# All steps of the kernel traced in one explicit order under a manual schedule

## The chip, the cores and the metric

The kernel runs on one NeuronCore of one Trainium2 chip, as one program with one launch. The metric is the device time of that core in microseconds (us); the time of a kernel is the median of several executions. The engines are TensorE (PE, with its weight loads listed apart as PEld), VectorE (DVE), ScalarE (ACT), GpSimd (POOL) and SyncE (SP), whose queue here issues all transfers. Each engine works through its own queue of instructions in order; between engines there are only semaphores.

## The reference

Three layers follow each other, for 8 independent batches of 576 positions and 512 channels (8 heads of 64):

```
# 1. attention over a memory of 32 slots per head
a    = softmax(phi, over the 576 positions)              # phi: 8 heads x 576 x 32
k_m, v_m = a^T k, a^T v                                  # 32 x 64 per head
x    = softmax(q k_m^T / 8) v_m                          # 576 x 64 per head, heads side by side
# 2. a mix over positions of rank 32, then an MLP, both with a residual
u    = x + (x^T U V)^T
y    = u + max(u w_ch1, 0) w_ch2                         # 512 -> 2048 -> 512
# 3. causal attention of 4 experts with 64 channels each, the two best by a gate
w    = softmax over the 2 largest of y w_gate, else 0
out  = sum_e w_e * (softmax(causal(q_e k_e^T / 8)) v_e wo_e),   q_e, k_e, v_e = y wq_e, y wk_e, y wv_e
```

Inputs and output are float32. The kernel writes every float32 operand of a matmul as the sum of two float16 numbers, hi and lo, and forms each product as hi*hi + hi*lo + lo*hi, so that one product of the reference is three matmuls.

## The kernel before, in words

**Steps.** The work of one batch is cut into steps, which are Python functions; most are generators, and what lies between two `yield` statements is a *segment*: a few instructions, mostly of one engine. Stage 1 (L542) has for each of four pairs of heads `pair_max`, `pair_scale`, `pair_hl` (the split into hi and lo, L661 to L673), `pair_qT` (a transposing DMA), `pair_kv` (L693), `pair_kb`, `pair_scores` (L729), `soft_a` and `soft_b`, and for each two pairs `half_t` (a transposing DMA), `half_p` and `half_a` (L904); `u_max` (L971) ends it with the largest magnitude over the whole tile. Such a maximum over all rows goes through PE each time: DVE fills a diagonal (L246) and a matmul with ones spreads it (L256, named `ur` after `u_max`, `ar` after `pair_max`, `yr` after `y_max`). `u_scale` and `a_split` scale and split the result, `u_mm` (L1054) forms u, and `zed` (L1078) folds the first weights of the MLP with the values of stage 1 so that the batches 1 to 7 need fewer products in `up`.

`mlp` (L1111) goes twice through 8 units of `up` (L1136, into one PSUM bank each, evicted as a hi part by ACT L1138 and a lo part by DVE L1140) and 4 of `down` (L1150, added to u by DVE L1157) for each half of the positions. `stage2` (L1178) takes the maximum (`y_max`), scales and splits y (`y_split`, L1230), and projects it (`proj` L1240, `vg` L1276). For each of five tiles of 128 positions and each pair of experts, `unit_s` forms scores on PE, then DVE masks them and takes their minimum (L1364), ACT takes the exponential (L1370) and a float16 copy (L1371), POOL forms the lo part (L1373), and SP issues a transposing DMA (L1375); `unit_v` (L1428) multiplies by the values, `unit_o` scales and transposes the result, `unit_w` (L1507) projects it and ACT evicts it (L1515).

**Buffers.** PSUM has three pools of banks: three banks with tag m (L175) for `up` and `down`, four with tag a (L178) for nearly everything else, and one with tag v (L181) for `unit_v`. A step that needs a bank waits until the one traced before it in that pool's ring has been read.

**Stages.** From the start the weights are loaded, converted and split (`w1_conv`, `w1_split`, `w2_conv`, `w2_split`, `sw_max`, `sw_split`) while batch 0 runs through stage 1 and its MLP. From then on a period holds `mlp` of batch b, `stage2` of batch b-1, and stage 1 of batch b+1, all mixed. In the end the MLP of batch 7 runs beside stage 2 of batch 6, and stage 2 of batch 7 runs alone.

**What sets the order.** Two things, one after the other. First a heap of events (`at` L1585, `run` L1589): each step gets a modelled time by hand (the constants UNIT, T0, LEAD, ZT, U_MM), and its segments are traced in the order of these times, each `yield` giving how much later the next segment follows. In the first part some weight steps are pinned behind the main work with `issue_after`. Then the framework's planner takes the traced instructions and reorders them in each engine's queue, by its own model of durations. The two last batches are traced from a text of step names, `ORDER2` (L1561, L1698 to L1702), and that part too goes through the planner. Where six matmuls in a row should stay in their order, as in `u_mm` and in the scores, the helper `in_order` (L305) chains them with `issue_after`, and the two banks of such a pair are taken in reversed order (`[::-1]`).

Of the kernel before, what the change touches and what calls it, by code (L numbers as in the profile page):

```python
# [53 lines left out]
ORDER2 = """  # L54
vg.P.0 y_max.P y_max.P y_scale.P y_scale.P y_split.P.0.0 y_split.P.0.0 y_split.P.0.3 y_split.P.0.3 y_split.P.1.2
y_split.P.1.2 y_scale.P y_split.P.0.2 y_split.P.1.3 up.0.0 up.0.1 up.0.0 up.0.0 up.0.1 y_split.P.1.0 y_split.P.0.1
y_split.P.0.1 up.0.1 up.0.2 up.0.3 y_split.P.0.2 up.0.2 up.0.2 y_split.P.1.0 u_mm.0.0 u_mm.0.0 u_mm.0.1 u_mm.0.1 up.0.4
up.0.4 proj.P.1.0.0 proj.P.1.0.0 up.0.3 proj.P.1.0.0 up.0.5 proj.P.0.0.0 up.0.4 up.0.3 up.0.5 proj.P.1.0.0 up.0.5 up.0.6
up.0.7 down.0.0.0.0 up.0.6 up.0.6 vg.P.1 up.0.7 up.0.7 down.0.0.0.1 down.0.0.1.0 y_split.P.1.1 y_split.P.1.1
y_split.P.1.3 proj.P.1.0.1 down.0.0.1.1 down.0.0.2.0 proj.P.1.0.1 vg.P.2 proj.P.0.0.0 vg.P.1 down.0.0.0.1 down.0.0.1.1  # L60
proj.P.0.0.0 down.0.0.2.1 vg.P.1 down.0.0.3.0 vg.P.2 vg.P.0 proj.P.1.0.0 proj.P.1.0.1 down.0.0.3.1 unit_s.P.0.0.0 vg.P.4
vg.P.2 vg.P.0 proj.P.1.0.1 proj.P.1.0.1 unit_s.P.0.0.1 vg.P.4 unit_s.P.0.0.0 unit_s.P.0.0.0 unit_s.P.0.0.0 vg.P.0 vg.P.3
vg.P.3 vg.P.3 down.0.0.3.1 down.0.0.2.1 unit_s.P.0.0.1 unit_s.P.0.0.1 unit_s.P.0.0.0 unit_s.P.0.0.0 proj.P.0.0.1 up.1.0
up.1.1 up.1.0 vg.P.4 unit_s.P.0.0.0 unit_s.P.1.0.0 proj.P.0.0.1 proj.P.0.0.1 up.1.2 up.1.1 unit_s.P.0.0.1 unit_s.P.0.0.1
unit_s.P.0.0.1 up.1.0 gate.P unit_o.P.0.0 unit_s.P.1.0.1 up.1.3 unit_s.P.1.0.0 up.1.1 unit_s.P.1.0.0 unit_s.P.1.0.0
up.1.2 up.1.2 unit_s.P.1.0.1 gate.P gate.P unit_o.P.0.0 gate.P unit_s.P.0.0.1 u_mm.1.0 u_mm.1.0 u_mm.1.1 u_mm.1.1 up.1.4
up.1.3 gate.P unit_v.P.0.0.0 up.1.3 up.1.4 up.1.5 unit_s.P.2.0.1 up.1.5 up.1.4 gate.P up.1.5 up.1.6 up.1.6 up.1.7 up.1.7
down.1.0.0.0 up.1.6 up.1.7 unit_s.P.3.0.0 unit_s.P.2.0.1 unit_s.P.2.0.1 gate.P unit_s.P.1.0.0 unit_s.P.1.0.0
unit_s.P.1.0.0 gate.P gate.P down.1.0.0.1 down.1.0.0.1 down.1.0.1.0 unit_v.P.0.0.1 unit_s.P.1.0.1 down.1.0.1.1
down.1.0.2.0 unit_s.P.1.0.1 unit_s.P.3.0.0 gate.P unit_o.P.0.0 unit_s.P.2.0.1 unit_o.P.0.0 unit_s.P.3.0.0 unit_s.P.1.0.1  # L70
unit_s.P.1.0.1 unit_v.P.1.0.0 down.1.0.1.1 unit_s.P.1.0.1 down.1.0.2.1 down.1.0.3.0 unit_s.P.2.0.0 unit_o.P.0.0
unit_s.P.2.0.0 unit_v.P.1.0.1 down.1.0.3.1 unit_s.P.3.0.1 unit_s.P.2.0.0 unit_s.P.2.0.0 unit_s.P.2.0.0 down.1.0.3.1
unit_s.P.2.0.0 unit_s.P.2.0.0 down.1.0.2.1 up.0.8 up.0.8 unit_s.P.2.0.1 unit_s.P.2.0.1 up.0.8 unit_s.P.3.0.1
unit_o.P.1.0 unit_o.P.1.0 up.0.9 up.0.9 up.0.9 unit_o.P.0.0 unit_o.P.1.0 unit_o.P.1.0 unit_o.P.1.0 up.0.10 up.0.10
unit_s.P.3.0.1 unit_o.P.2.0 unit_o.P.2.0 up.0.11 unit_v.P.2.0.0 up.0.11 up.0.11 unit_s.P.3.0.0 unit_s.P.3.0.0 up.0.10
# [74 lines left out]
def kernel(ctx: ExitStack, tc: tile.TileContext, q, k, v, phi, U, V, w1, w2, wg, wq, wk, wv, wo, out):  # L150
# [154 lines left out]
    def in_order(calls):  # L305
        last = None
        for f in calls:
            with tc.issue_after(last) if last is not None else nullcontext():
                f()
# [1430 lines left out]
```

## Time and profile before

| | |
|---|---|
| median of 3 runs | 1311.68 us (1308.8 to 1317.54) |
| the profiled execution's own time | 1309.13 us |
| its span, first to last instruction | 1307.1 us |
| mean granted clock of PE, 1 is full speed | 0.956 |
| busy share of the span: PE, DVE, ACT, POOL | 88%, 72%, 60%, 31% |
| DMA | 137.8 MB, 105 GB/s on average |

The durations quoted further on all come from the profiled execution, 2.6 us under the median. A busy engine is one that executes an instruction, so 88% says that PE had nothing to execute in 12% of the span; it does not say that the matmuls ran at the highest speed, since the granted clock sets their pace. PEld is the loading of weights, which overlaps with matmuls. DVE, ACT and POOL evict PSUM, split numbers into hi and lo and take maxima and exponentials.

### The profile page before, as it was taken

Reading aid. Unit: us, or ns where it says so; the run is one execution under the profiler, and the core shown is the slowest. Engines: PE = TensorE matmul, PEld = TensorE weight load, DVE = VectorE, ACT = ScalarE, POOL = GpSimd, SP = SyncE. Lnnn points to the kernel's source line nnn. Section 1 sums busy time; section 2 is a strip of 40 time slices with the busy share of each in tenths; the row PEclk is TensorE's granted clock in tenths of the full one; section 3 lists DMA queues with packets and bytes.
Section 4 is the critical chain, followed back from the end, with each engine's and each line's share of the span. In section 5 each row is a group of like instructions: output and inputs, shape, how many; then the busy total and the mean of one; then the engine's idle time right before and its main releaser. Section 6 shows DMA issues by size and latency. Waiting matters only on the chain. (4 is left out here: it accounts for less than half of the span.)

```text
span 1307.1 us, 29401 instructions
## 1 busy us (share of the span) xinstructions
PE 1148.9 (88%) x10961; PEld 819.9 (63%) x10961; DVE 935.7 (72%) x2876; ACT 781.6 (60%) x1899; POOL 410.9 (31%) x408
## 2 busy tenths in 40 slices
...
GB/s 241 246 145 172 113 78 69 50 116 117 87 74 107 104 100 104 144 59 95 139 76 118 92 103 110 136 71 90 121 82 136 77 106 78 143 20 54 49 66 124
DMA packets 268991, 137.77 MB, mean 105 GB/s; under 512 B 204880, under 2 KB 253712, under 8 KB 268848
## 3 DMA queue, kind: packets, MB, share of 16 engines
...
q14 instruction: 57, 0.47, 0.1%
...
## 5 line engine op out<-in xcount | busy, mean ns | idle before, releaser
L1150 PE MATMUL dn<-h,w2s 128*128 128x288 f16 x3072 | 412.1, 288 | 6.6 <-DVE h L1140 3.5
L1150 PEld LDWEIGHTS <-w2s 128*128 128x128 f16 x3072 | 292.0, 98 | 92.9 <-issue 19.2
L1373 POOL TENSOR_TENSOR phl<-pr,phl 128x128 f16<-128x128 f32 (+3 forms) x112 | 88.5, 790 | 312.3 <-ACT phl L1371 223.5
L1140 DVE SCALAR_TENSOR_TENSOR h<-up,h 128x288 f16<-128x288 f32 x256 | 111.7, 450 | 52.9 <-ACT h L1138 52.1
L1136 PEld LDWEIGHTS <-w1s 128*128 128x128 f16 x1056 | 104.9, 103 | 53.1 <-issue 22.2
L1138 ACT ACTIVATE h<-up 128x288 f16<-128x288 f32 x256 | 99.5, 405 | 49.1 <-PE up L1136 44.4
L673 POOL TENSOR_TENSOR kvq<-raw,kvq 96x768 f16<-96x768 f32 x48 | 78.4, 1642 | 144.8 <-ACT raw L667 143.0
L640 DVE TENSOR_REDUCE amax<-raw 96x1 f32<-96x768 f32 x72 | 67.9, 944 | 55.3 <-DMA raw<-in_v_dram 31.1
L1370 ACT ACTIVATE pr<-sc,nm 128x128 f32<-128x128 f32 (+3 forms) x112 | 58.8, 525 | 76.4 <-DVE nm L1364 44.2
L1136 PE MATMUL up<-ahl,z 128*128 128x288 f16 x672 | 99.9, 296 | 3.5 <-DVE h L1140 3.0
L1136 PE MATMUL up<-ahl,w1s 128*128 128x288 f16 x672 | 97.1, 290 | 6.5 <-DVE h L1140 6.3
L1136 PEld LDWEIGHTS <-z 128*128 128x128 f16 x672 | 64.8, 101 | 30.8 <-issue 11.7
L1364 DVE CUSTOM_DVE_ANT_0 sc<-sc,wmask,ysc 128x128 f32<-128x128 f32 (+3 forms) x128 | 66.9, 553 | 20.0 <-PE sc L1348 19.4
L1428 PE MATMUL av<-vhl,pT 128*128 128x64 f16 (+2 forms) x1050 | 62.9, 199 | 16.5 <-DMA pT<-phl 13.0
L1428 PEld LDWEIGHTS <-pT 128*128 128x128 f16 (+1 forms) x1050 | 49.9, 98 | 39.2 <-DMA pT<-phl 23.1
L1136 PE MATMUL up<-uhl,w1s 128*128 128x288 f16 x384 | 60.3, 323 | 10.7 <-DVE u L1157 6.8
L661 ACT ACTIVATE kvq<-raw,ps 96x768 f16<-96x768 f32 x72 | 62.5, 925 | 8.1 <-DVE ps L269 3.2
L1484 ACT ACTIVATE ohl<-av,fac 128x64 f16<-128x64 f32 (+1 forms) x140 | 37.7, 307 | 43.9 <-PE av L1428 20.2
L1507 PE MATMUL wo<-wos,oT 128*128 128x512 f16 (+1 forms) x288 | 57.0, 356 | 2.7 <-ACT oT L1477 2.2
L1371 ACT ACTIVATE phl<-pr 128x128 f16<-128x128 f32 (+3 forms) x112 | 52.4, 468 | 3.6 <-DMA pT<-phl 1.6
L1091 PE MATMUL z<-w1s,vz 128*64 128x512 f16 x336 | 51.5, 414 | 1.2 <-DMA w1s<-w1d 1.0
L1157 DVE SCALAR_TENSOR_TENSOR w1s<-dn,us,w1s 128x288 f32<-128x288 f32 x64 | 32.5, 508 | 25.0 <-PE dn L1150 24.4
...
## 6 DMA issues: line engine op xcount, KB each, us to landing
...
```

The lines of the kernel that those rows point to most:

```text
L640: dve.tensor_reduce(o, raw, axis=AX.XYZ, op=ALU.max, apply_absolute_value=True)
L661: act.activation(hl[:, 0], src, AF.Copy, scale=s[0:SP, j:j + 1])
L673: pool.tensor_tensor(hl[:, 1], src, hl[:, 0], op=ALU.subtract)
L1136: pe.matmul(pm, lhs, uhl[c][:, kc], start=(kc + a + c == 0), stop=(a == 1 and kc == (1 if b else KC - 1)))
L1138: act.activation(hb[:, 0, g], pm, AF.Relu)
L1140: dve.scalar_tensor_tensor(hb[:, 1, g], pm, 0.0, hb[:, 0, g], op0=ALU.max, op1=ALU.subtract)
L1150: pe.matmul(pm, w2s[:, m, fg, a, g], hb[:, c, g], start=(g == 0 and a + c == 0), stop=(g == FG - 1 and a == 1))
L1364: dve.tensor_tensor_reduce(psc[:, 0:n], psc[:, 0:n], wmask[:, (NT - 2 - i) * P:(NT - 1) * P], cs, 3.0e38, ALU.add, ALU.min, nm)
L1370: act.activation(pr[:, 0:n], psc[:, 0:n], AF.Exp, bias=nm, scale=-1.0, accum_out=ss[:, eo:eo + 1])
L1373: (dve if tail and TD >> (2*i + eo) & 1 else pool).tensor_tensor(phl[:, n:2 * n], pr[:, 0:n], phl[:, 0:n], op=ALU.subtract)
L1428: pe.matmul(pav[:, eo * D:(eo + 1 + last) * D], pT[:kn, a * (i + 1) + j], vhl[:kn, c, j, vs], start=(j == 0 and a + c == 0), stop=(j == i ...
L1507: pe.matmul(pw[g * n:g * n + n, 0:W], oT[:, a, 0:n], wos[:, c, ep, g * W:(g + 1) * W], start=(c_ == 0), stop=(c_ == 5))
```

## The change

The text `ORDER2`, the heap of events with its modelled times, and the helper `in_order` go. In their place stands one text `ORDER` with 5679 names of steps, from the first load to the last store. A name appears once for each of a step's segments that has a place of its own; `advance` runs the next segment of the named step each time, and runs what is left of a step at its last mention. All of it is traced inside `tc.manual_schedule()`, where the framework's planner does nothing: the order of tracing is the order in each engine's queue, SP's with its DMA issues included. The places in `ORDER` come from list scheduling with durations measured in traces. The step functions are the same, apart from the plain loops in `u_mm` and in the scores and the two banks in plain order. The name `setup.close` in the text stands for the release of the buffers of the first part.

```diff
-        o = [ps_a(f"u{b}_{hf}_{a}_{pp}")[:, 0:NH] for pp in range(2)][::-1]
+        o = [ps_a(f"u{b}_{hf}_{a}_{pp}")[:, 0:NH] for pp in range(2)]
...
-            return lambda: pe.matmul(o[pp], vth[r, x], ahl[y][r, hf], start=(n_ == 0), stop=(n_ == 2))
-
-        in_order([product(n_, x, y, pp) for n_, (x, y) in enumerate(((0, 0), (0, 1), (1, 0))) for pp in range(2)])
+            pe.matmul(o[pp], vth[r, x], ahl[y][r, hf], start=(n_ == 0), stop=(n_ == 2))
+
+        for n_, (x, y) in enumerate(((0, 0), (0, 1), (1, 0))):
+            for pp in range(2):
+                product(n_, x, y, pp)
...
-    events = []
-    made = []
-    main = {e: [] for e in (dve.engine, act.engine, pe.engine)}
-
-    def at(t, f, *a, fill=False):
-        heapq.heappush(events, (t, len(made), f, a))
-        made.append([None, fill])
...
+    plan = {}
+    gens = {}
+
+    def put(f, *a, of=None):
+        plan[".".join([f.__name__] + [str(x) for x in (() if of is None else (of,)) + a])] = f, a
+
+    def puts(steps, b):
+        for _, f, a in steps:
+            put(f, *a, of=b)
+
+    def advance(order):
         left = {}
         for k_ in order:
             left[k_] = left.get(k_, 0) + 1
...
+        for k_ in order:
+            if k_ not in gens:
+                f, a = plan.pop(k_)
+                gens[k_] = f(*a) or iter(())
+            next(gens[k_], None)
+            left[k_] -= 1
+            if not left[k_]:
+                go(gens[k_])
...
+    with tc.manual_schedule():
+        first, _, second = ORDER.partition("setup.close")
+        advance(first.split())
+        setup.close()
+        for b in range(NB):
+            puts(stage2(b), b)
+        advance(second.split())
+    assert not plan
```

Some places of `ORDER`. In a name the first number is the batch; `up.3.1.0` is batch 3, second half of the positions, first unit. The first lines are from the start, the next three parts from the period of batch 3 into that of batch 4, and the last part from the second half of stage 2 of batch 7:

```diff
+w2_conv.2 w2_load.1 half_u.0.1.1 phi_max.1 w1_load.6 w2_conv.2 u_max.0 w2_conv.4 w2_conv.2 u_max.0 w1_conv.5 phi_max.1
+w2_conv.4 u_scale.0 w2_conv.4 u_scale.0 phi_max.1 u_split.0.0 u_scale.0 w2_conv.2 w2_conv.2 w1_conv.5 u_split.0.1
+u_split.0.0 phi_max.1 w2_conv.4 phi_sub.1.0 u_split.0.1 up.0.0.0 w2_split.2 w2_load.3 phi_sub.1.1 phi_sub.1.0
+w2_conv.4 up.0.0.1 w2_split.2 w1_conv.5 up.0.0.0 up.0.0.2 up.0.0.1 w2_conv.6 up.0.0.0 up.0.0.1 w1_conv.5 up.0.0.3
...
+unit_s.2.1.0.0 gate.2 gate.2 down.3.0.0.3.1 pair_scale.4.2 gate.2 gate.2 unit_s.2.1.0.0 gate.2 unit_s.2.1.0.1
+unit_s.2.1.0.1 unit_s.2.1.0.0 unit_s.2.1.0.0 unit_s.2.1.0.0 pair_kv.4.1 gate.2 pair_scale.4.2 gate.2 down.3.0.0.3.1
+unit_s.2.1.0.0 gate.2 raw_load.4.4.3.0 pair_scale.4.2 unit_v.2.0.0.0 unit_o.2.0.0 up.3.1.0 unit_o.2.0.0 pair_kb.4.1
+unit_s.2.1.0.1 unit_s.2.1.0.1 unit_s.2.1.0.1 unit_s.2.1.0.0 pair_kb.4.1 pair_kb.4.1 up.3.1.1 up.3.1.0 unit_s.2.1.0.1
+pair_scores.4.1 unit_o.2.1.0 up.3.1.0 up.3.1.1 pair_kb.4.1 unit_s.2.1.0.1 up.3.1.1 up.3.1.2 soft_a.4.1 pair_scores.4.1
+soft_a.4.1 up.3.1.3 up.3.1.2 pair_scores.4.1 pair_scores.4.1 soft_a.4.1 unit_v.2.0.0.1 unit_s.2.2.0.0 up.3.1.2
+pair_scores.4.1 soft_b.4.1 up.3.1.4 unit_o.2.0.0 unit_s.2.2.0.0 pair_scores.4.1 up.3.1.3 up.3.1.5 soft_b.4.1 up.3.1.4
...
+unit_v.2.0.1.0 unit_o.2.0.1 unit_o.2.0.1 down.3.0.1.2.1 half_p.4.1 phi_load.5.5.0 half_p.4.1 half_p.4.1 unit_s.2.1.1.1
+half_a.4.1 down.3.0.1.2.1 phi_load.5.5.1 unit_v.2.0.1.1 unit_s.2.2.1.0 half_a.4.1 unit_o.2.0.1 down.3.0.1.3.0
+half_a.4.1 unit_s.2.2.1.0 u_max.4 unit_o.2.0.1 unit_s.2.2.1.0 unit_s.2.2.1.0 unit_s.2.2.1.0 zed.4.0.0.1 u_max.4
+unit_o.2.0.1 unit_o.2.0.1 unit_s.2.2.1.1 unit_s.2.2.1.1 down.3.0.1.3.1 zed.4.0.0.1 u_scale.4 unit_s.2.2.1.0 u_scale.4
+u_scale.4 z_load.4.1.0.0 a_split.4.0 zed.4.0.0.1 unit_s.2.2.1.0 unit_s.2.2.1.1 unit_s.2.2.1.1 unit_s.2.2.1.1
+unit_v.2.1.1.0 unit_o.2.1.1 a_split.4.0 up.3.1.8 down.3.0.1.3.1 unit_w.2.0 unit_o.2.2.1 up.3.1.8 unit_s.2.2.1.1
...
+unit_w.2.3 phi_rm.5 down.3.1.1.3.1 unit_w.2.3 unit_w.2.3 up.4.0.0 down.3.1.1.3.1 up.4.0.1 up.4.0.0 up.4.0.0 u_mm.4.0.0
+up.4.0.1 y_max.3 up.4.0.2 y_max.3 u_mm.4.0.0 up.4.0.1 pair_max.5.1 u_mm.4.0.1 up.4.0.2 up.4.0.3 u_mm.4.0.1
+pair_max.5.0 y_scale.3 up.4.0.3 unit_w.2.4 y_scale.3 pair_scale.5.0 y_split.3.0.0 unit_w.2.4 u_mm.4.1.0 y_scale.3
+y_split.3.0.1 pair_scale.5.0 up.4.0.4 y_split.3.0.0 pair_hl.5.0.2 pair_scale.5.0 up.4.0.2 zed.4.1.0.1 y_split.3.0.2
+y_split.3.0.1 pair_hl.5.0.2 pair_hl.5.0.2 up.4.0.5 pair_hl.5.0.0 z_load.5.0.0.0 y_split.3.0.3 y_split.3.0.2
+raw_load.5.5.1.1 pair_hl.5.0.0 up.4.0.3 y_split.3.0.3 up.4.0.6 pair_qT.5.0 y_split.3.1.0 pair_hl.5.0.0 u_mm.4.1.0
...
+unit_o.7.4.0 unit_o.7.2.0 unit_s.7.2.1.0 unit_w.6.4 unit_w.7.0 unit_s.7.1.1.1 unit_s.7.2.1.0 unit_s.7.3.1.0
+unit_s.7.2.1.1 unit_s.7.2.1.1 unit_s.7.2.1.0 unit_s.7.2.1.0 unit_s.7.2.1.0 unit_o.7.4.0 unit_w.6.4 unit_v.7.0.1.1
+unit_o.7.3.0 unit_s.7.3.1.0 unit_s.7.2.1.1 unit_s.7.2.1.1 unit_s.7.2.1.1 unit_s.7.2.1.0 unit_s.7.3.1.1 unit_s.7.3.1.1
+unit_s.7.3.1.0 unit_s.7.3.1.0 unit_s.7.3.1.0 unit_o.7.0.1 unit_s.7.2.1.0 unit_s.7.2.1.1 unit_o.7.0.1 unit_v.7.1.1.0
+unit_v.7.1.1.1 unit_o.7.4.0 unit_s.7.3.1.1 unit_s.7.3.1.1 unit_s.7.3.1.1 unit_o.7.4.0 unit_s.7.2.1.1 unit_s.7.3.1.0
+unit_w.7.1 unit_o.7.0.1 unit_s.7.3.1.0 unit_o.7.1.1 unit_s.7.3.1.1 unit_o.7.4.0 unit_o.7.0.1 unit_o.7.2.1 unit_o.7.1.1
+unit_o.7.1.1 unit_w.7.0 unit_o.7.1.1 unit_s_last.7.1 unit_o.7.4.0 unit_w.7.0 unit_s.7.3.1.1 unit_v.7.2.1.0
```

## Rows read from the trace of the kernel before

**Rows 1.** The page's busy line: us, share of the span, instructions.

```profile
PE 1148.9 (88%) x10961; PEld 819.9 (63%) x10961; DVE 935.7 (72%) x2876; ACT 781.6 (60%) x1899; POOL 410.9 (31%) x408
```

**Rows 2.** Busy table by stretch: us, busy us (count) PE, PEld, DVE, ACT, POOL, PEclk, DMA, GB/s.

```profile
0.00:78.80 78.80, 41.11 (x263) 30.20 (x264) 60.07 (x151) 45.97 (x78) 35.30 (x36) 0.86 0.87 246
78.80:237.90 159.10, 130.08 (x1086) 95.54 (x1086) 128.44 (x293) 92.97 (x159) 71.73 (x44) 0.86 0.38 103
237.90:385.90 148.00, 133.93 (x1261) 94.43 (x1260) 110.71 (x349) 87.11 (x212) 42.79 (x45) 0.93 0.38 84
385.90:533.30 147.40, 135.57 (x1361) 97.02 (x1361) 108.63 (x350) 91.65 (x232) 45.82 (x48) 0.99 0.46 103
533.30:686.60 153.30, 140.08 (x1361) 98.28 (x1361) 110.03 (x354) 92.05 (x233) 45.77 (x48) 0.96 0.46 106
686.60:831.60 145.00, 133.41 (x1355) 96.32 (x1354) 107.67 (x348) 90.87 (x231) 45.70 (x48) 1.00 0.48 102
831.60:983.70 152.10, 138.06 (x1356) 97.39 (x1355) 109.63 (x353) 92.10 (x232) 45.83 (x48) 0.97 0.47 106
983.70:1124.00 140.30, 131.08 (x1344) 95.22 (x1343) 102.22 (x341) 90.35 (x231) 45.61 (x48) 1.00 0.42 93
1124.00:1307.10 183.10, 165.59 (x1589) 115.50 (x1585) 98.28 (x347) 98.52 (x298) 32.34 (x43) 1.00 0.34 76
```

**Rows 3.** Waits of PE, 237.9 to 1124.0 us: us in total, times, longest us.

```profile
PE ur L256 <- DVE dg L246: 12.6, 5, 2.8
PE av L1428 <- DMA pT<-phl: 11.5, 16, 2.0
PE up L1136 <- DVE h L1140: 8.8, 7, 2.7
PE ar L256 <- DVE dg L246: 6.9, 5, 2.4
PE ss L729 <- DMA pT<-phl: 6.6, 4, 1.8
PE a L904 <- DMA aT<-ah: 5.6, 5, 2.7
PE u L1065 <- ACT ob L1515: 5.3, 8, 0.9
```

**Rows 4.** Timeline of PE from 720 to 751 us: start, duration, group of instructions.

```profile
725.06 1.63 PE L1136 MATMUL up<-ahl,z 128*128 128x288 f16 x12
726.53 1.50 PE L1276 MATMUL vg<-wvg,yhl 128*128 128x260 f16 x12
727.86 1.21 PE L693 MATMUL kv<-e,kvq 96*128 96x64 f16 x36
```

**Rows 5.** The page's costliest groups: busy us, mean ns of one, idle before.

```profile
L1373 POOL TENSOR_TENSOR phl<-pr,phl 128x128 f16<-128x128 f32 (+3 forms) x112 | 88.5, 790 | 312.3 <-ACT phl L1371 223.5
...
L1138 ACT ACTIVATE h<-up 128x288 f16<-128x288 f32 x256 | 99.5, 405 | 49.1 <-PE up L1136 44.4
...
L1370 ACT ACTIVATE pr<-sc,nm 128x128 f32<-128x128 f32 (+3 forms) x112 | 58.8, 525 | 76.4 <-DVE nm L1364 44.2
...
L1364 DVE CUSTOM_DVE_ANT_0 sc<-sc,wmask,ysc 128x128 f32<-128x128 f32 (+3 forms) x128 | 66.9, 553 | 20.0 <-PE sc L1348 19.4
...
L1371 ACT ACTIVATE phl<-pr 128x128 f16<-128x128 f32 (+3 forms) x112 | 52.4, 468 | 3.6 <-DMA pT<-phl 1.6
```

**Rows 6.** One line's instructions, 237.9 to 1124.0 us: ns min/median/max, first and last start.

```profile
L1140 DVE SCALAR_TENSOR_TENSOR h<-up,h x192: 414/448/459, 241.2 to 1103.9; 128x288 f16<-128x288 f32 x192
...
L1230 DVE SCALAR_TENSOR_TENSOR yhl<-u,ysc,yhl x24: 527/532/2059, 250.8 to 865.9; 128x288 f16<-128x288 f32 x24
...
L1375 SPq DMA_TRANSPOSE pT<-phl x94: 1167/1211/2608, 276.4 to 1122.5; - x94
DMA to landing us min/median/max: 2.3/3.0/5.2
```

**Rows 7.** Busy table of one stretch of the last batch, columns as in rows 2.

```profile
1144.00:1242.00 98.00, 96.86 (x896) 72.44 (x895) 49.73 (x166) 45.98 (x138) 14.45 (x20) 1.00 0.22 41
```

More of the change, by code (lines that the diff above doesn't have):

```diff
@@ L64 @@
[L64 to L68, printed above, removed]
@@ new lines @@
+phi_es.4.1 phi_split.4.1 unit_o.1.4.1 unit_o.1.4.1 unit_w.1.3 unit_o.1.4.1 unit_o.1.4.1 phi_sum.4 pair_max.4.0
+raw_load.4.4.1.0 unit_w.1.3 phi_rm.4 down.2.1.1.3.1 unit_w.1.3 unit_w.1.3 up.3.0.0 down.2.1.1.3.1 up.3.0.1 up.3.0.0
+up.3.0.0 u_mm.3.0.0 up.3.0.1 y_max.2 up.3.0.2 y_max.2 u_mm.3.0.0 up.3.0.1 pair_max.4.1 u_mm.3.0.1 up.3.0.2 up.3.0.3
+u_mm.3.0.1 pair_max.4.0 y_scale.2 up.3.0.3 unit_w.1.4 y_scale.2 pair_scale.4.0 y_split.2.0.0 unit_w.1.4 u_mm.3.1.0
+y_scale.2 y_split.2.0.1 pair_scale.4.0 up.3.0.4 y_split.2.0.0 pair_hl.4.0.2 pair_scale.4.0 up.3.0.2 zed.3.1.0.1
@@ new lines @@
+phi_split.7.0 unit_o.4.3.1 unit_w.4.2 down.5.1.1.2.1 phi_sub.7.1 unit_o.4.3.1 unit_o.4.3.1 unit_o.4.3.1 vg.5.0
+unit_v.4.4.1.0 unit_o.4.4.1 unit_o.4.4.1 phi_split.7.1 down.5.1.1.2.1 raw_load.7.7.0.2 down.5.1.1.3.0 phi_es.7.1
+phi_split.7.1 unit_o.4.4.1 unit_o.4.4.1 unit_w.4.3 unit_o.4.4.1 unit_o.4.4.1 phi_sum.7 pair_max.7.0 raw_load.7.7.1.0
+unit_w.4.3 phi_rm.7 down.5.1.1.3.1 unit_w.4.3 unit_w.4.3 up.6.0.0 down.5.1.1.3.1 up.6.0.1 up.6.0.0 up.6.0.0 u_mm.6.0.0
+up.6.0.1 y_max.5 up.6.0.2 y_max.5 u_mm.6.0.0 up.6.0.1 pair_max.7.1 u_mm.6.0.1 up.6.0.2 up.6.0.3 u_mm.6.0.1
@@ L302, in words @@
         return ap.bitcast(U32).rearrange("a (n t) -> a n t", t=2)
[L305 to L309, printed above, removed]
-            last = next(i for i in reversed(nc.cur_bb.bb.instructions) if i.engine == pe.engine)
     st = {}
@@ L1646 @@
+    put(uv_load)
+    put(u_setup)
+    put(v_setup)
+    for c in range(NC1):
+        put(w1_load, c)
+        put(w1_conv, c)
+        put(w1_split, c)
+        put(w1_store, c)
+        put(w2_load, c)
+        put(w2_conv, c)
+        put(w2_split, c)
     for x in range(2):
-        at(T0 + LATER + 26 + 3 * x, zed, 1, 0, x, 0, fill=None)
-        at(T0 + LATER + 47 + 3 * x, zed, 1, 0, x, 1, fill=None)
-    for n in range(2):
-        at(T0 + 50 + 3.5 * n, sw_load, n)
+        put(w1_scale, x)
+        put(sw_load, x)
```

835 lines of the change are left out of this document (626 added, 209 removed).

## The prediction

> **What bounds the kernel now.** First the page's busy line [rows 1]: TensorE (PE) is busy for 88% of the span, VectorE (DVE) 72%, ScalarE (ACT) 60%, GpSimd (POOL) 31%. So PE is the engine nearest to a bound, and the question is where its other 158 us lie. An average over the span can't say that, so I cut the span where `up` of each batch begins and read the busy table of these stretches [rows 2]. The reader is to see three regimes. From 0 to 237.9 us (weights are converted, batch 0 runs, batch 1 is prepared) PE is idle for 37.7 + 29.0 us and its clock is 0.86; here DVE is busy 60.1 + 128.4 = 188.5 us of 237.9, more than any other engine. From 237.9 to 1124.0 (batches 1 to 6, one period each) PE is busy 812.1 of 886.1 us, so 74.0 us are idle, some 12 per period; DVE is busy 102 to 111 us per period, ACT 87 to 92. After 1124.0 (batch 7, no later batch to prepare) PE idles 17.5 us.
>
> Then the list of who PE waited for, in the six periods [rows 3]: seven kinds of wait make 57.3 of the 74.0 us, and none of them is a shortage. Each is a matmul that stands too early in PE's queue behind something that ends a little later: a maximum over rows (L256), a transposing DMA, an eviction. The chain of waits on the page ends at its last two steps and tells nothing here; the cause has to come from the waits.
>
> The clock is the second loss. The period with clock 1.00 that does the full work has PE busy 133.4 us; those with 0.99, 0.96 and 0.97 have 135.6, 140.1 and 138.1 for the same number of matmuls within 0.5% [rows 2]. That is 2.2 + 6.7 + 4.7 = 13.6 us of slower matmuls, in the periods that idle 11.8 to 14.0 us.
>
> **The change, part by part.** No matmul, no operation and no DMA is added or removed: the step functions are the same. What changes is the place of every instruction in its engine's queue, those of SP (all DMA issues) included. So each term is a wait of before, and whether the new list leaves enough PE work between the producer and the consumer. I price PE work by three neighbouring rows: 12 matmuls of 288 columns take 1.47 us from start to start, 12 of 260 columns 1.33 [rows 4]; the smaller ones by their columns.
>
> *Six periods, waits.* Batch 4 of the list, whose neighbours look alike:
> - L256 `ur` (12.6 us): between the second `half_a` and the maximum the list puts one `down` half and most of a `zed`, 2.7 us, and 30 us more before `up` of that batch. I take 10 off.
> - `av` behind the transposed probabilities (11.5 us, 16 times): the chain is DVE 0.55, ACT 0.53 and 0.47, POOL 0.79 [rows 5] and a landing of 3.0 us [rows 6], 5.3 in all. The list keeps 8.3 to 15 us of PE work between score matmuls and `unit_v`. 9 off.
> - `up` behind DVE's half of an eviction (8.8): the three `up` banks come round after 1.7 to 5 us of PE work, the two evictions take 0.41 [rows 5] and 0.45 [rows 6]. 6 off.
> - L256 `ar` (6.9): 4 off, an estimate; a matmul of one row of maxima is placed right behind its planned producer.
> - `ss` behind the transposed q (6.6): 10 to 19 us now lie between. 6 off.
> - `a` behind the transposed attention (5.6): 6.3 us for the first half, but only 2.6 for the second, against a landing near 3.0. 3 off.
> - `u` behind the output eviction (5.3): the bank comes round after 12 us. 5 off. But at the start of each batch four pairs of `u_mm`, `y_max`, `pair_max`, the last `unit_w` and a `zed` share four banks with 0.9 to 2.1 us between uses; I charge 0.5 us per period, 3 us, about one eviction of 0.41.
> The sum is 43 - 3 = 40 us off, of 74. The bounds are 0 (every wait comes back elsewhere) and 74.
>
> *Six periods, clock.* With half of the idle time gone the lower clock has fewer occasions; I take 8 of 13.6, bounds 0 and 13.6.
>
> *Start.* The list moves conversions of weights 4 and 5 ahead of the first `up`, into 0 to 78.8 us where DVE has 18.7 us free, and so takes them out of 78.8 to 237.9, where PE idles 29.0 us and runs at 0.86. PE's own time there is 130.1 us at that clock, DVE's 128.4, in 159.1. I take 20 off, two thirds of that idle time. Bounds: nothing (DVE work that only changes places), and 45, which would leave 193 us, just over DVE's 188.5. In the first 78.8 us I take nothing off: the DMA engines are 87% busy there.
>
> *End.* The old list of the last two batches gave PE idle times of 17.5 us. The new list for batch 7 leaves 3.8 to 8 us of PE work between scores and `unit_v` in its second half, against the chain of 5.3: it is short there too. 5 off, bounds 13 off and 6 on.
>
> *Edits with one answer.* The helper that chained the score matmuls one behind the other goes, and the pairs of banks are no longer reversed: in a list the order traced is the order issued, so both cost and bring nothing. SP: per period some 74 issues by the code, 34 of them transposes at 1.21 us [rows 6], which is 41 us of 148; the queue has room, but a waiting issue now holds those that the list put behind it. I charge nothing for it in the sum, because the distances above exceed the chains; the price if that cover is gone is the second rival's.
>
> Sum: 40 + 8 + 20 + 5 = 73 us. The profiled execution took 1309.1 (span 1307.1 and 2.0 around it), 2.6 below the median of the runs, 1311.7. 1309.1 - 73 = **1236 us**. With bounds less extreme together than singly the forecast's own range is 1205 to 1262.
>
> What speaks for planning by measured durations is how narrow the commonest are in the six periods: 192 evictions of `up` on DVE took 414 to 459 ns [rows 6]. A planned queue misses only where a duration isn't one number.
>
> **Rivals.**
> *DVE becomes the bound (chance 0.17, 1262 to 1290).* For it: with periods of 133 us DVE's 109 would be 82% of the time in a queue that can't step aside, and in the old periods it also sat idle 39 us each. If periods stay at 143, six of them give 28 us, and with 10 from the start the time is 1309 - 38 = 1271. Here a duration does vary: L1230, which reads two tensors from SBUF beside POOL's work, took 527 to 2059 ns, median 532 [rows 6]. If all 48 took the longest, DVE would work 1.53 x 48 = 73 us more, 12 per period, 121 of 133. Against it: the median is near the minimum, so few were held up. The Trainium skill's "SBUF — State Buffer", section "Who interferes with whom", says that a DVE instruction with two SBUF inputs and a GpSimd instruction that reads SBUF exclude each other for a whole instruction. By that rule a tighter schedule meets it more often; the longest L1230 agrees with it, the median shows that it is rare so far.
>
> *Slower: transposes land later than planned (0.08, 1300 to 1345).* The place is `unit_v` on PE, 126 of them, each behind one transposing DMA on SP. Landings took 2.3 to 5.2 us and an issue 1.17 to 2.61 [rows 6]. If SP, where loads that wait for a buffer now hold fixed places, makes each transpose late beyond its 3 to 10 us of slack, PE waits in order at each: 0.72 us apiece (11.5 / 16) is 91 us, and 1236 + 91 = 1327. It decides from 73 / 0.72 = 101 of the 126. Against it: in the old trace 16 of 108 waited, with less care taken.
>
> *No change (0.07, 1300 to 1318).* Waits only change places: the old queues were also a fixed order by the time the kernel ran, and 92% PE busy in the periods leaves little. Against it: the waits of [rows 3] have named causes, and the list separates them.
>
> *Better: PE nearly without idle time (0.13, 1165 to 1205).* 74 off, 14 of clock, 30 from the start and 8 at the end give 1309 - 126 = 1183. For it: in the last batch there are stretches of 100 us with PE busy for nearly all of it [rows 7]. Against it: there DVE was busy only half the time. The Trainium skill's "Perfetto Trace Analysis", "Identifying the Most-Contended Engine", says that matmul busy time is a poor measure of the distance to the limit and weight loads a better one. By weight loads, some 96 us per period against 133 [rows 2], even more than 126 us would be free; I found no row in which the kernel comes near that.
>
> **How the numbers follow.** Forecast 0.55, DVE bound 0.17, better 0.13, slower 0.08, no change 0.07. The likeliest case gives 1236. The range 1180 to 1295 takes in the forecast, nearly all of the DVE case and the upper half of the better one, about 8 in 10. A measurement of this kernel can tell about 1%, 13 us. Faster by more: 0.55 + 0.17 + 0.13 = 0.85; within: 0.07; slower: 0.08.
>
> **What would show it.** In the changed profile: periods between the first `up` of batches of 135 to 140 us with PE idle 4 to 7 us in each; no L256 `ur` wait above 1 us; `av` behind DMAs in total under 4 us; clock 0.98 or more from the first `up` of batch 1; that `up` near 218 us. DVE idle under 20 us per period, with PE waiting for DVE, would show the first rival, `av` behind DMAs as PE's largest wait the second. I am wrong if PE's idle time in the periods stays above 60 us.

## The result, and the profile after

The changed kernel takes 1254.96 us (median of 4 runs, 1252.25 to 1255.39) against 1312.05 before (median of 4 runs beside them): a ratio of 0.9556, 95% interval 0.9521 to 0.9592, or 57 us less. The forecast was 1236, 73 us off the profiled execution. The profiled execution of the changed kernel has a span of 1250.5 us, 56.6 less than that of before. The page's busy line, as [rows 1]:

```profile
PE 1115.3 (89%) x10961; PEld 810.4 (65%) x10961; DVE 937.0 (75%) x2876; ACT 795.5 (64%) x1899; POOL 409.9 (33%) x408
```

The counts are the same: nothing was added or removed. PE is busy 33.6 us less, although it executes the same matmuls, so the idle time went down by only 56.6 - 33.6 = 23.0 us. The share of 89% hides both. The busy table cut where `up` of each batch begins, as [rows 2]:

```profile
0.00:88.30 88.30, 40.86 (x263) 31.17 (x264) 69.36 (x153) 49.04 (x76) 37.92 (x38) 0.86 0.75 210
88.30:237.60 149.30, 123.45 (x1091) 92.84 (x1090) 127.95 (x305) 96.91 (x165) 68.45 (x42) 0.92 0.43 116
237.60:384.10 146.50, 136.13 (x1357) 96.88 (x1356) 114.89 (x358) 98.03 (x239) 54.09 (x54) 0.98 0.49 110
384.10:522.20 138.10, 131.28 (x1356) 95.53 (x1355) 108.83 (x352) 93.26 (x231) 45.95 (x48) 1.00 0.49 114
522.20:662.20 140.00, 132.73 (x1356) 96.06 (x1354) 108.07 (x350) 93.22 (x231) 45.62 (x48) 0.99 0.50 110
662.20:802.00 139.80, 132.83 (x1356) 96.04 (x1355) 107.98 (x350) 93.22 (x231) 45.62 (x48) 0.99 0.50 110
802.00:942.70 140.70, 132.69 (x1356) 96.30 (x1355) 107.89 (x350) 92.93 (x231) 45.57 (x48) 0.99 0.49 109
942.70:1079.70 137.00, 131.46 (x1362) 95.63 (x1361) 99.88 (x338) 89.42 (x226) 38.04 (x43) 1.00 0.47 101
1079.70:1250.50 170.80, 153.84 (x1478) 109.91 (x1476) 92.14 (x326) 89.46 (x269) 28.61 (x39) 0.98 0.28 60
```

Read against [rows 2]: the first `up` of batch 1 is where it was (237.6 after, 237.9 before). The six periods take 842.1 us instead of 886.1, with 45.0 us of idle PE time instead of 74.0. The end is 12.3 us shorter, but it has 111 matmuls fewer; its idle time is the same (17.0, was 17.5). The periods, in turn, hold 103 matmuls more. At the 0.104 us per matmul of the old end (165.59 / 1589) that is some 11 us of work which moved forward. So on equal work the periods won some 55 us (an estimate, since the matmuls that moved are not of the mean size), and the start and the end next to nothing.

Who PE waited for in the six periods, as [rows 3]:

```profile
PE pmr L1116 <- DVE pmd L1114: 8.6, 4, 2.2
PE up L1682 <- DVE h L1686: 6.8, 12, 1.2
PE es L1157 <- POOL es L1155: 5.5, 5, 1.2
PE ar L807 <- DVE dg L797: 5.1, 8, 1.2
PE a L1448 <- DMA aT<-ah: 2.8, 2, 1.5
PE yr L807 <- DVE dg L797: 2.3, 2, 2.0
PE av L1975 <- DVE ohl L2035: 2.2, 4, 0.6
PE pj L1786 <- ACT u L1616: 2.1, 3, 1.4
PE vg L1822 <- ACT u L1616: 2.1, 3, 0.8
PE vg L1822 <- ACT w1s L1616: 1.5, 2, 0.9
```

Line 807 is what was L256, 1682 was L1136, 1975 was L1428. `ur`, `ss` behind its DMA, `av` behind its DMA and `u` behind ACT are gone. In their place stand `pmr`, `es` and `yr`, and waits for the banks that `u_mm` had filled. They recur at the same places: `pmr` waits 2.15 us in each of batches 4 to 7. Waits at one place in every period are what a fixed order leaves.

### The profile page after: what moved, and what is told of

Read it like the earlier page. It is cut to its first block, busy times and chain, and to the rows that moved or that the text cites. A ratio compares the mean times of both kernels' runs of the same rounds, so it can differ in the third digit from the quotient of the medians.

```text
span 1250.5 us, 29433 instructions
## 1 busy us (share of the span) xinstructions
PE 1115.3 (89%) x10961; PEld 810.4 (65%) x10961; DVE 937.0 (75%) x2876; ACT 795.5 (64%) x1899; POOL 409.9 (33%) x408
## 5 line engine op out<-in xcount | busy, mean ns | idle before, releaser
L1682 PEld LDWEIGHTS <-w1s 128*128 128x128 f16 x1056 | 103.1, 101 | 46.4 <-issue 15.5
L1911 DVE CUSTOM_DVE_ANT_0 sc<-sc,wmask,ysc 128x128 f32<-128x128 f32 (+3 forms) x128 | 68.5, 551 | 10.8 <-PE sc L1894 10.3
L2054 PE MATMUL wo<-wos,oT 128*128 128x512 f16 (+1 forms) x288 | 61.2, 357 | 2.2 <-ACT oT L2024 1.4
L1975 PE MATMUL av<-vhl,pT 128*128 128x64 f16 (+2 forms) x1050 | 58.3, 199 | 2.2 <-DVE ohl L2035 2.2
L1822 PE MATMUL vg<-wvg,yhl 128*128 128x260 f16 (+1 forms) x504 | 47.9, 256 | 3.6 <-ACT u L1616 2.1
```

The costliest lines, as they stand in the source:

```text
L1682: pe.matmul(pm, lhs, uhl[c][:, kc], start=(kc + a + c == 0), stop=(a == 1 and kc == (1 if b else KC - 1)))
L1911: dve.tensor_tensor_reduce(psc[:, 0:n], psc[:, 0:n], wmask[:, (NT - 2 - i) * P:(NT - 1) * P], cs, 3.0e38, ALU.add, ALU.min, nm)
L1975: pe.matmul(pav[:, eo * D:(eo + 1 + last) * D], pT[:kn, a * (i + 1) + j], vhl[:kn, c, j, vs], start=(j == 0 and a + c == 0), stop=(j == i ...
L2054: pe.matmul(pw[g * n:g * n + n, 0:W], oT[:, a, 0:n], wos[:, c, ep, g * W:(g + 1) * W], start=(c_ == 0), stop=(c_ == 5))
```

## The experiments

The table is in the order of the sections below; the first `up` of batch 1 and the four periods (first `up` of batch 3 to that of batch 7) are read from the traces. Ratios are against the kernel before on the same chip.

| kernel | ratio, 95% interval | median us | first up of batch 1 | four periods |
|---|---|---|---|---|
| changed | 0.9556 [0.9521, 0.9592] | 1255.0 | 237.6 | 557.5 |
| list replanned | 1.0030 [1.0003, 1.0058] | 1314.2 | 249.3 | 595.4 |
| start replanned | 0.9641 [0.9602, 0.9679] | 1263.7 | 250.0 | 555.7 |
| before, plain loops | 0.9892 [0.9844, 0.9940] | 1296.9 | 236.5 | 585.6 |
| ur early | 0.9657 [0.9622, 0.9693] | 1265.6 | 237.8 | 560.2 |
| pmr later | 0.9508 [0.9468, 0.9547] | 1247.4 | 240.5 | 551.0 |
| three later | 0.9520 [0.9476, 0.9563] | 1248.0 | 238.4 | 552.8 |
| lone matmuls, slipped | 0.9732 [0.9692, 0.9772] | 1276.3 | 240.2 | 571.7 |
| lone matmuls, 32 | 0.9563 [0.9513, 0.9613] | 1253.9 | 235.4 | 554.5 |
| conversions back | 0.9602 [0.9570, 0.9635] | 1258.4 | 243.6 | 555.6 |
| no POOL addition | 0.9425 [0.9380, 0.9469] | 1235.0 | 221.8 | 557.2 |
| DVE work to POOL | 0.9608 [0.9564, 0.9652] | 1260.2 | 244.5 | 556.8 |
| no lo parts on DVE | 0.9514 [0.9462, 0.9567] | 1246.7 | 229.8 | 557.4 |

The six kernels whose start is untouched (changed, ur early, pmr later, three later, both with lone matmuls) have their first `up` of batch 1 between 235.4 and 240.5, and the six with untouched periods (changed and the five with an edit of the start alone) take 555.6 to 557.5 us for the four periods. That is the scatter against which the others are read.

### The list without the manual schedule

```diff
-    with tc.manual_schedule():
+    with nullcontext():
         first, _, second = ORDER.partition("setup.close")
```

> The changed kernel with the same list of names, traced outside the manual schedule, so that the framework's planner reorders every queue by its own durations. If the gain lies in the queues as the list sets them, it goes with them: 1295 to 1325 us, the six matmuls of a score pair apart again in a third of the pairs (the changed kernel has them together in all), and PE waits of 2 us or more behind maxima over rows, each followed by a stretch at the lower clock. Rival: the list alone, as the order of tracing, carries the gain, and the planner changes little: 1250 to 1275 us.

The gain is gone, 1.003. Its waits of PE in the periods, two lines:

```profile
PE av L1975 <- DMA pT<-phl: 22.8, 19, 2.9
PE up L1682 <- DVE h L1686: 10.5, 12, 2.3
```

The planner, given the same list to trace, puts `unit_v` too early again, twice as badly as before [rows 3]. Of the groups of score matmuls 51 runs were of three, so the pairs were apart. What gained is the queue as the list has it, not the list as an order of tracing: under the planner the list is even 17 us slower than the old order with the same plain loops (the kernel before with plain loops, below, 1296.9). No run issued the old order without the planner, so what the manual schedule would do for that order stays open. Of the waits behind maxima that I expected, `ar` is there (7.8 us, up to 3.9 at a time) and `ur` is not; the waits behind DMAs I had not expected.

### The first part replanned

```diff
-    with tc.manual_schedule():
-        first, _, second = ORDER.partition("setup.close")
-        advance(first.split())
-        setup.close()
+    first, _, second = ORDER.partition("setup.close")
+    advance(first.split())
+    setup.close()
+    with tc.manual_schedule():
```

> Only the first part of the list (up to the release of the first part's buffers) is left to the planner; the rest keeps its manual order. If the first part is bound by the work of DVE, whose busy time was 188.5 of 237.9 us before and 197.3 of 237.6 us after, then its order is worth little: the first up of batch 1 at 232 to 245 us and the time 1247 to 1265 us. Rival: the manual order hides a real gain of the first part behind the extra work that it pulls in, and without it the time rises by 10 us or more, to 1265 to 1285 us.

The first `up` of batch 1 comes 12.4 us later and the time is 9 us longer by the medians (0.9641 against 0.9556, 11 us). The first `up` misses the theory's range by 5 us; the time, 1263.7, is at the upper end of the theory's range and 1.3 us under the rival's. So for this list the manual order of the first part is worth some 10 us, as the rival said. But it only reaches what the old hand-set times reached with the planner, 237.9.

### One part of the change alone, in the kernel before

```diff
-            with tc.issue_after(last) if last is not None else nullcontext():
-                f()
-            last = next(i for i in reversed(nc.cur_bb.bb.instructions) if i.engine == pe.engine)
+            f()
...
-        o = [ps_a(f"u{b}_{hf}_{a}_{pp}")[:, 0:NH] for pp in range(2)][::-1]
+        o = [ps_a(f"u{b}_{hf}_{a}_{pp}")[:, 0:NH] for pp in range(2)]
```

(the same for the two other pairs of banks)

> The kernel before with one part of the change alone: the six matmuls in plain loops, without the chain of issue_after, and the banks in plain order; the planner stays. I had booked this part at nothing. If it is worth nothing by itself: 1305 to 1317 us. If the planner, no longer held by the chain, parts the pairs into two threes, as it did in the list that was replanned: slower by 5 to 15 us, 1316 to 1328 us. If the chain itself was what let lone matmuls slip in: faster by 5 to 12 us, 1298 to 1306 us.

0.9892, 13 us, the third case and a little more. Of the six matmuls the planner now made 63 runs of three, and yet it is faster: this gain does not come from pairs that stand together. In its waits from 236.5 to 1114.6 us there is no line for `ur` at all (12.6 us before) nor for `ss` behind a DMA (6.6), while `av` went up:

```profile
PE av L1426 <- DMA pT<-phl: 16.1, 20, 2.0
PE up L1134 <- DVE h L1138: 10.4, 18, 2.5
PE a L902 <- DMA aT<-ah: 6.1, 8, 1.3
```

So in the old kernel the chain of `issue_after` (or the reversed banks; the run does not part the two) bought waits elsewhere in PE's queue.

### A wait put back: ur early

```diff
+        for b in range(2, NB - 1):
+            x = [i for i, n in enumerate(order) if n in (f"half_a.{b}.1", f"u_max.{b}")]
+            names = [order[i] for i in x]
+            for i in x[:0:-1]:
+                del order[i]
+            order[x[0] + 1:x[0] + 1] = names[1:]
```

> In batches 2 to 6 the segments of the second half_a and of u_max follow each other directly, so that the matmul that spreads the maximum (ur) stands in PE's queue right behind its producers, as in the kernel before. Each then waits some 2.5 to 3.5 us, five times. Theory: a wait of that length costs more than itself, since the granted clock falls to its lower level for some us behind it (in the changed kernel 1.7 us of lost clock stand behind each of the three 2.15 us waits for pmd that I looked at): 5 x (3 + 1.7) = 23 us, 1270 to 1285 us, with three to five new stretches of lower clock. Rival 1: the wait costs itself alone, 10 to 17 us, 1265 to 1272, clock as before the edit. Rival 2: DVE and ACT use the time to get ahead and it is given back, 1252 to 1260.

```profile
PE ur L807 <- DVE dg L797: 9.8, 5, 2.0
PE pmr L1116 <- DVE pmd L1114: 8.6, 4, 2.2
```

9.8 us of wait came back and the span grew by 10.6 (1261.1), the median by the same: a wait on PE costs itself, rival 1. It is not given back, and on balance it did not cost more: the six periods of the run together have PE busy for 797.87 us, 797.12 in the changed kernel. The waits came out at 1.96 us instead of 2.5 to 3.5.

### A wait taken away: pmr later

In `phi_max` the diagonal on DVE and the matmul `pmr` were one segment, so no list could part them. Here is a `yield` between them, and the matmul has its own place:

```diff
+            if b > 3:
+                yield
             pm = ps_a(f"pmr{b}")
...
+        for b in range(4, NB):
+            del order[[i for i, n in enumerate(order) if n == f"phi_max.{b}"][4]]
+            order.remove(f"unit_w.{b - 3}.2")
+            z = order.index(f"zed.{b - 1}.1.1.0")
+            order[z + 1:z + 1] = [f"unit_w.{b - 3}.2"] + [f"phi_max.{b}"] * 2
```

> In the changed kernel the segment of phi_max that fills the diagonal on DVE holds the matmul pmr too, so the list can't put anything between them; PE waits 2.15 us there in each of batches 4 to 7. Here the matmul is a segment of its own, behind one zed and one unit_w (about 1.6 us of PE work). Theory: the order can take this wait away too, what stood in the way was the cut into segments: 4 x 1.7 to 2.15 = 7 to 9 us, and up to 1.7 us more for each stretch of lower clock that goes with it: 1240 to 1248 us. Rival: the chain behind pmr (ACT, POOL phi_sub, then the sum es, where PE waits 1.23 us) is late by as much, and the wait moves to es or further: 1251 to 1258 us.

The four periods, in this kernel and then in the changed one (columns as in rows 2):

```profile
525.10:1076.10 551.00, 525.62 (x5425) 382.74 (x5424) 424.58 (x1386) 367.81 (x919) 174.66 (x187) 1.00 0.48 109
```

```profile
522.20:1079.70 557.50, 529.71 (x5424) 384.04 (x5422) 423.83 (x1385) 368.79 (x919) 174.86 (x187) 0.99 0.49 107
```

6.5 us less, of which 4.1 is PE's busy time (the clock) and 2.4 idle time. The `pmr` wait fell from 8.6 us to 1.0, but the wait of the last tile's values for their bank grew:

```profile
PE av L1977 <- DVE ohl L2037: 6.5, 8, 1.1
PE es L1159 <- POOL es L1157: 5.5, 5, 1.2
```

The time, 1247.4, is at the upper end of the theory's range. The rival has a part of it: `es` did not move, but 4.3 of the 7.6 us taken off at `pmr` came back at `av` (2.2 to 6.5). This kernel is faster than the one before and than the changed one, 0.9508, and the shorter periods (551.0 where the untouched ones scatter from 555.6 to 557.5) say so more sharply than the overlapping intervals.

### Three waits taken away

```diff
+            order.remove(f"phi_rm.{b}")
+            d = order.index(f"down.{b - 2}.1.1.3.1")
+            order[d + 1:d + 1] = [f"phi_sum.{b}", f"phi_rm.{b}"]
+            y = order.index(f"unit_v.{b - 3}.4.1.0")
+            late = order[y:y + 3]
+            del order[y:y + 3]
+            d = order.index(f"down.{b - 2}.1.1.3.0")
+            order[d + 1:d + 1] = late
```

(with a `yield` in `phi_sum` ahead of its matmul)

> The kernel with pmr in a segment of its own, and in batches 4 to 7 two more matmuls moved later by 1.5 to 3 us of PE work: es (cut off from the POOL addition in front of it; PE waited 1.23 us there in each period) and the values of the last tile (PE waited 1.05 us there for the release of the one bank they use). Theory: these are waits of place too, 4 x (1.23 + 1.05) = 9 us at most, 1238 to 1243 us. Rival: what was moved is late for its own consumers, and the waits go on to the next place, as half of the gain at pmr did: 1243 to 1250 us.

```profile
PE ar L807 <- DVE dg L797: 8.3, 10, 2.9
PE up L1685 <- DVE h L1689: 5.6, 11, 1.0
PE yr L807 <- DVE dg L797: 3.6, 5, 2.0
...
PE up L1685 <- DVE w1s L1706: 2.4, 2, 1.2
PE wo L2057 <- DMA oT<-ohl: 2.3, 4, 1.6
```

Nothing further was gained over the kernel with `pmr` alone, the rival's case: `es` fell to 0.6 us and `av` to 2.2, but `ar` rose by 2.9, `yr` by 1.0, and `up` behind DVE's addition and `unit_w` behind its DMA are new. Here one wait became the next.

### Score groups with a lone first matmul

After the change the six matmuls of a score group stand together, two by two on the two halves of the rows; before, 36 runs of the score line were of one. Two kernels issue the first matmul of a group one step ahead, as the old queue did.

```diff
                 for eo in range(2):
                     product(n_, x, y, eo)
+                    if not tail and n_ + eo == 0:
+                        yield
```

> In 32 of the 56 score groups of batches 0 to 6 (tiles 0 to 3) the first of the six matmuls is issued alone, ahead of one other step on PE, as the planner had done in about a third of the groups of the kernel before; the other five follow at their old place. Theory: the two matmuls of a pair, on the two halves of the rows, run side by side (in the changed kernel the second starts 4 ns behind the first), and a lone one pays for itself and for its partner: 0.1 to 0.25 us per group, the score matmuls of the six periods 3 to 7 us longer from start to start, the time 1257 to 1263 us. Rival: a lone matmul is hidden like any other, 1253 to 1256 us.

All 56 groups were split, not 32, and in 24 of them what followed slipped by one place; the expectation did not foresee that. Hence the second kernel, with the `yield` in the 32 groups alone:

> As the run with lone first matmuls, but now in 32 score groups only, and the 24 others are left as they are: there the run before had split all 56, and in 24 the five matmuls that remained, and what followed them, had slipped by one place. In that run the score matmuls of the six periods (48 groups) took 10.6 us longer from start to start, 0.22 us per group. Theory: this price alone counts, 32 x 0.22 = 7 us, 1259 to 1265 us; the other 12 us of the run before were the slipped places. Rival: a lone first matmul costs more than its own time, since DVE gets its scores later: 1266 to 1278 us.

The timeline of PE at one group, with the lone matmul, then in the changed kernel:

```profile
697.56 0.28 PE L1894 MATMUL sc<-kh,qh 64*128 64x256 f16 x1
697.77 1.64 PE L1696 MATMUL dn<-h,w2s 128*128 128x288 f16 x12
699.25 0.29 PE L807 MATMUL ar<-dg,onesb 96*128 96x288 bf16 x1
699.47 0.28 PE L1894 MATMUL sc<-kh,qh 64*128 64x256 f16 x1
699.48 0.39 PE L1894 MATMUL sc<-kl,qh 64*128 64x256 f16 x2
699.60 0.38 PE L1894 MATMUL sc<-kh,ql 64*128 64x256 f16 x2
699.90 1.64 PE L1696 MATMUL dn<-h,w2s 128*128 128x288 f16 x12
```

```profile
701.38 0.28 PE L1894 MATMUL sc<-kh,qh 64*128 64x256 f16 x2
701.50 0.27 PE L1894 MATMUL sc<-kl,qh 64*128 64x256 f16 x2
701.61 0.27 PE L1894 MATMUL sc<-kh,ql 64*128 64x256 f16 x2
701.81 1.40 PE L1696 MATMUL dn<-h,w2s 128*128 128x288 f16 x10
```

The five take as long as the six (699.90 - 699.47 = 0.43 us and 701.81 - 701.38 = 0.43), so the lone one costs its whole 0.21 us. Summed from each score matmul's start to that of the next matmul on PE, the scores of the six periods took 42.6 us against 37.1. Yet the time did not change (0.9563): theory and rival were both wrong. PE's idle time in the six periods fell from 45.0 to 40.9 us: the work stood ahead of waits that became shorter (`pmr` 1.84 us each time for 2.15, `up` 5.3 us in all for 6.8). PE's busy time rose by only 2.5 us (799.6 for 797.1), because no wait at `pmr` was followed by the lower clock here. The 22 us between the two kernels lie in the 24 groups that slipped: their own lone matmuls can make up some 5 us of it (24 x 0.21, an estimate), the rest is the slipped places and what hung on them.

### The first part: what bounds it

Four edits, each of the start alone. First, the conversions that the list had put ahead of the first `up` go back:

```diff
+        u = order.index("up.0.0.0")
+        late = [n for n in order[:u] if n in ("w1_conv.4", "w1_conv.5", "w1_load.6")]
+        order = [n for n in order[:u] if n not in late] + order[u:]
+        u = order.index("up.0.0.4")
+        order[u + 1:u + 1] = late
```

> The conversion of weights 4 and as much of 5 as stood ahead of the first up goes back behind the fifth up of batch 0 (with the load of weights 6, which takes the same buffer). If DVE bounds the first part, the first up of batch 0 comes 4 to 7 us earlier than the changed kernel's 88.3 us, the first up of batch 1 stays within 3 us of 237.6, and the time within 4 us of 1255. Rival: the conversions ahead of the first up are the loss that I had booked as a gain, and the time falls with them by 5 to 9 us, to 1246 to 1250.

The first `up` of batch 0 came 1.8 us earlier (86.5), that of batch 1 6.0 later, 3 outside the scatter of the untouched starts. The time, 1258.4, is within the theory's 4 us, but the two `up` are not where it put them, and the rival is refuted: the conversions ahead are a gain, of some 3 to 6 us, as the prediction had it, but a fraction of its 20.

(The weights of the MLP, U and V arrive as 64-bit numbers, which the section on the reference leaves out; the conversions put each together from two 32-bit halves.)

```diff
-        pool.tensor_tensor(z.bitcast(I32), z.bitcast(I32), lo.bitcast(I32), op=ALU.add)
+        pool.tensor_tensor(z.bitcast(I32)[:, 0:32], z.bitcast(I32)[:, 0:32], lo.bitcast(I32)[:, 0:32], op=ALU.add)
```

> Leaves out most of the POOL addition in the conversion of the weights (32 of its columns stay), so the weights miss their low bits; 18 POOL instructions of about 2.4 us become short ones. Theory: DVE bounds the first part, and part of its time is waiting for the memory beside POOL (the same 128x1024 DVE instruction took 1.21 to 3.02 us): DVE's busy time up to the first up of batch 1 falls from 197 us by 8 to 20, that up comes 6 to 15 us before 237.6, the time is 1240 to 1249 us. Rival: the stretched instructions are not on the path, only the fixed order is: within 3 us of 1255.

```diff
-SP1 = 17476
-SP2 = 1028
+SP1 = 26214
+SP2 = 42662
```

> The ten lo parts of the weights of the MLP that DVE forms (16 us of its time in the first part) are formed by POOL instead, with a scaled copy by ACT; all is computed. Theory: DVE bounds the first part, so it gets shorter, by 5 to 14 us: first up of batch 1 at 224 to 233 us, 1241 to 1250 us. Rival: POOL's 20 us more stretch DVE's other instructions by as much and ACT's ten copies stand in the way of evictions: no gain or a loss, 1253 to 1270 us.

```diff
-            dve.scalar_tensor_tensor(lo, z, s, hi, op0=ALU.mult, op1=ALU.subtract)
+            dve.memset(lo, 0.0)
```

> Leaves out the lo parts of the weights that DVE forms (a memset to zero stands in their place), so DVE loses some 14 us of its 197 before the first up of batch 1, and POOL and ACT get nothing instead. Theory 1: DVE alone bounds the first part, so the first up of batch 1 comes 9 to 15 us before 237.6 and the time is 1240 to 1247 us. Theory 2: POOL bounds it together with the fixed order (taking 35 us from POOL gave 16 us, taking 13 us from DVE and giving POOL 17 lost 7): that up within 4 us of 237.6 and the time 1250 to 1258 us.

The stretch up to the first `up` of batch 1: changed kernel, no POOL addition, DVE work to POOL, no lo parts (columns as in rows 2):

```profile
0.00:237.60 237.60, 164.31 (x1353) 124.01 (x1354) 197.31 (x457) 145.94 (x241) 106.37 (x80) 0.90 0.55 151
```

```profile
0.00:221.80 221.80, 164.76 (x1353) 123.62 (x1354) 182.87 (x457) 145.30 (x241) 71.33 (x80) 0.90 0.59 162
```

```profile
0.00:244.50 244.50, 167.25 (x1354) 124.42 (x1354) 184.50 (x447) 156.76 (x251) 123.49 (x90) 0.88 0.53 147
```

```profile
0.00:229.80 229.80, 162.03 (x1353) 122.45 (x1354) 183.16 (x457) 145.42 (x241) 100.75 (x81) 0.90 0.56 156
```

Taking 14.2 us from DVE gave 7.8 (POOL's time fell by 5.6 with it); taking 35.0 from POOL, without touching an instruction of DVE, shortened DVE's own work by 14.4 and gave 15.8; moving 12.8 from DVE to POOL, with 10.8 more on ACT, lost 6.9. Without POOL's addition the time, 1235.0, came out below the theory's range of 1240 to 1249, and its rival is refuted; the work moved to POOL is the rival's case. So the first part is bound by the work of DVE and POOL, and not by DVE alone: of the last run's theories the first has the time (1246.7) but overstates the first `up` (7.8 us earlier for 9 to 15), the second is refuted. What share each engine's time has, and whether ACT's ten copies made the loss, stays open.

## Why the prediction was right, and where it was not

*The mechanism* was right: waits of place go when the queue is set with room between producer and consumer, and most of the lower clock went with them. That 57 us came out against 73 is in part luck, since large errors in the terms ran against each other: 20 us of the start and most of 5 at the end did not come, new waits took 21 where 3 were charged, while the clock and a term that had been put at nothing gave back more PE time than forecast. Of the signs named beforehand the waits and the clock came as stated and the periods nearly so (137.0 to 140.7 us from the second on, idle 5.5 to 8.0 us; the first 146.5 and 10.4); the first `up` of batch 1 near 218 did not. *Six periods, waits*: of the seven kinds I took 43 off; they fell from 57.3 to 14.7 us (`up` 6.8, `ar` 5.1, `a` 2.8, the rest at or near nothing), 42.6. Singly I was low on `ur` (12.6 for 10) and `av` (all 11.5 for 9) and high on `up` (2.0 for 6) and `ar` (1.8 for 4). What failed is the charge of 3 for new waits: `pmr` rose from 1.7 to 8.6, `es` is new with 5.5, `yr` with 2.3, and the banks behind `u_mm` cost 6.2 (the three lines above and one of 0.5), 21 us in all (the banks twice my 3). Other small waits went, and the net is 29.0 off instead of 40. I had looked for matmuls too near their producers in the list alone; `pmr`, `es`, `ar` and `yr` sit in one segment with their producers, where no list can part them (so does `ur`, which no longer waits), and parting one, `pmr`, was worth 6.5 us in the four periods.

*Six periods, clock*: 8 forecast. Length times what is missing to clock 1.00, summed over the six rows, gives 22.5 us before and 7.1 after, so some 15 came back at most (idle time under the lower clock is counted too); my bound of 13.6 had left out the first period. The condition was too simple as well: the old period with clock 1.00 idled 11.6 us, as much as the one with 0.99 (11.8).

*Start* is the step that failed. I took 20 off, two thirds of PE's idle time, on the ground that DVE had 18.7 us free in the first 78.8. The first `up` of batch 0 came 9.5 us later, and that of batch 1 stayed. The bound "nothing" was the true value. The conversions moved ahead explain only 1.8 of the 9.5 us, as the edit back showed. The larger part was lost before them: the last `at` on POOL, with which the softmax of batch 0 ends and for which PE waits on its way to that `up`, starts 8.75 us later than before, with or without them (changed kernel, conversions back, kernel before):

```profile
63.83 1.67 POOL L1402 TENSOR_TENSOR at<-sx,ssm 96x384 f32<-96x384 f32 x1
63.86 1.67 POOL L1402 TENSOR_TENSOR at<-sx,ssm 96x384 f32<-96x384 f32 x1
55.08 1.16 POOL L858 TENSOR_TENSOR at<-sx,ssm 96x384 f32<-96x384 f32 x1 [2.42 <-DVE ssm L853]
```

From its end to the first `up` it is 22.9 us in the changed kernel and 22.6 in the one before. So the list lets batch 0 come late in this part; which of its places does that stays open. DVE and POOL hold the part together, and moving DVE's work ahead bought the 3 to 6 us that the edit back showed, no more.

*End*: 5 forecast. The stretch lost 12.3, but 111 matmuls with it; its idle time fell by 0.5.

*Edits with one answer*: that the chain of `issue_after` and the reversed banks cost nothing was wrong, for the kernel before: removing them alone gave 13 us there. Under the manual schedule that part can't be told apart; what manual schedule and list add to it is the rest, 1297 to 1255. A second term was put at nothing too. With all pairs together, from start to start and with idle time taken off, the score matmuls of the six periods took 36.2 us (432 of them) after 43.8 (415), and those of `u_mm` 11.7 after 15.5 (144): some 13 us less PE time for the same number. On equal work PE was busy some 26 us less in the periods (15.0, and 11 for the 103 matmuls more), so about half of that is the pairs and the rest mostly the clock. How much of the 13 us the time has is not shown: the 32 lone matmuls put 5.5 of it back, and the time stayed.

*The rivals*: transposes did not land late, `av` behind a DMA vanished. DVE did not become the bound of the periods: it is busy 108 of 140 us there. In the first part its conflict with POOL is real: with 35.0 us less POOL work its own instructions took 14.4 us less. The timeline of the changed kernel:

```profile
68.77 2.45 POOL L885 TENSOR_TENSOR w1s<-w2s,w1s 128x1024 f16<-128x1024 f32 x1
...
69.28 3.02 DVE L848 SCALAR_TENSOR_TENSOR w2z<-w2r,w2z 128x1024 uint32<-128x1024 uint32 x1
```

L848 took 1.21 us at its shortest in this kernel; here it starts 0.5 us after POOL's 2.45 us subtraction and ends 1.08 us behind it. The Trainium skill's "SBUF — State Buffer", "SBUF: two separate sides", says that a DVE instruction with two SBUF inputs, as this one, and a GpSimd instruction that reads SBUF exclude each other for a whole instruction. By that rule DVE waits out POOL's subtraction and then runs its 1.21 us; the 3.02 us agree with it.
